# A fused attention and gated-MLP kernel: its build-time scheduler places single instructions event by event instead of whole steps

## The chip, the cores and the metric

The kernel runs on one core of one Trainium2 chip. The metric is the device time of one execution in microseconds (us). The execution that was profiled is one such execution; its span runs from the first to the last instruction of the program and is a little shorter than its device time.

## The reference

The input x has 2048 tokens (S) of width 640 (D). After a layer norm over D, two branches read the same xn and both are added to x:

- attention in linear form with 32 heads of width 20: q, k and v from one weight `wqkv`; q and k each go through a small per-head matrix `w_phi`, then through a softmax over +p and one over -p, which are laid side by side (40 features a head);
- a gated MLP of inner width 1536 (F).

```python
pq = einsum("bhsd,hdf->bhsf", q, w_phi);  pk = einsum("bhsd,hdf->bhsf", k, w_phi)
phi_q = concat([softmax(pq), softmax(-pq)]);  phi_k = concat([softmax(pk), softmax(-pk)])
kv  = einsum("bhsf,bhsd->bhfd", phi_k, v);    z = sum over s of phi_k
o   = (phi_q @ kv) / ((phi_q . z) + 1e-6)
out = x + concat_heads(o) @ wo + (silu(xn @ w1) * (xn @ w3)) @ w2
```

So kv and z are sums over all 2048 tokens of the k side, and nothing of the q side can be finished before they are complete.

## The kernel before

Tokens lie in 16 tiles of 128 (t = 0 to 15) and in 4 blocks of 512 (b = 0 to 3). The program is one list of steps per engine, laid out when it is built. The steps, with the names that the trace uses:

- **norm** of tile t: two `bn_stats` and one `bn_aggr` on VectorE (DVE), eps and the power on GpSimd (POOL), the scaling of `x_tok` on DVE or ScalarE (ACT). Tiles 0 to 3 are transposed by TensorE (PE), tiles 4 to 15 by a DMA transpose on SP's queue (`xnT<-x_tok`).
- **fold(1)** and **fold(0)**: `w_phi` is multiplied into the k and q weights (`PS<-BDc,wqkT`), five pieces each; the results are `Wkp` and `Wqp`. POOL builds `BDc` from `phi_s`.
- **V** and **K** of tile t: 10 matmuls of 320 columns each (`PS<-wv,xnT`, `PS<-Wkp,xnT`). V is copied by ACT into `v2`; K goes through two Exp on ACT into `ekt`.
- **k_norm** of tile t: DVE sums (`S<-ekt`) and takes reciprocals (`rS<-S`), POOL multiplies (`ekt<-ekt,rS`, two instructions). `S` and `rS` have three buffers.
- **kv_sum**: 192 small matmuls over all 16 tiles (`PS<-ekt,v`), then a copy to `kvT`; **kv_back**: 24 small matmuls (`PS<-PT,kvT`), then `KVc` on DVE. Only then can attention go on.
- **Q** of block b, piece fc: 5 matmuls of 512 columns (`PS<-xnT,Wqp`), two Exp on ACT (`EqT`).
- **q_tok** of tile t: 20 small matmuls into four PSUM banks (`PS<-KVc,EqT`), two `e_s` copies on ACT, then six instructions on DVE (`pr_s`, `den_s` twice, `g_s`, `prod`, `o_tok`), then a DMA transpose to `oT`.
- **M** of block b, piece fc (48 in all): 10 matmuls of 512 columns into two banks (`PS<-xnT,w_s`; `w_s` stands for w1, w3 and w2 alike), a Tanh on ACT (`th`), two `scalar_tensor_tensor` on DVE (`t`, `hT`).
- **O** of tile t: 34 matmuls of 320 columns (`PS<-wo_s,oT` and `PS<-w_s,hT`), one add on DVE (`xres`), a store.

What sets the order: `_Program` keeps a modelled clock per engine. Nine streams (norms, x_dma, attention, k_norms, o_transposes, mlps, outs, stores, x_loads) offer one step each; the loop picks the step whose modelled start is earliest, `commit` appends **all** instructions of that step to their engines' lists, and the choice starts anew. PSUM banks are chosen by `banks(n)` as an aligned group of n, and a group is free when the last reader of any of its banks has ended. An engine runs its list strictly in order: an instruction that stands behind a waiting one waits too. PE starts with 21 dummy matmuls on a zero tile (`dummies`), before the first real work. Nearly every instruction is recorded by one helper, so the profile shows them all at line 104.

Of the kernel before, what the change touches and what calls it, by code (L numbers as in the profile page):

```python
# [9 lines left out]
D = 640  # L10
# [10 lines left out]
ENGINES = ("PE", "ACT", "DVE", "POOL", "SP")  # L21
GRAN = 32

# [5 lines left out]
TRIPLES = ((0, 3, 0, 60), (3, 3, 60, 60), (6, 3, 120, 60), (9, 3, 180, 60), (12, 3, 240, 60), (13, 3, 300, 20))  # L29


class _Op:
    __slots__ = ("name", "part", "eng", "emit", "reads", "writes", "cost", "dma", "deps", "start", "end",
                 "inc", "count", "sem", "clock", "idx")

    def __init__(self, eng, emit, reads, writes, cost, dma=False):
        self.eng, self.emit, self.reads, self.writes = eng, emit, reads, writes
        self.cost, self.dma = cost, dma
        self.name = ""
        self.part = False  # L40
        self.inc = False
        self.count = 0
        self.sem = None


class _Program:

    def __init__(self, nc):  # L50
        self.nc = nc
        self.eng = {"PE": nc.tensor, "ACT": nc.scalar, "DVE": nc.vector,
                    "POOL": nc.gpsimd, "SP": nc.sync}
        self.base = {}
        self.ops = []
        self.free = dict.fromkeys(ENGINES, 0.0)
        self.bus = 0.0
        self.last_w = {}
        self.last_r = {}
        self.bank = {}  # L60
        self.pending = None
        self.pool = None
# [6 lines left out]
    def regions(self, ap):  # L69
        if not hasattr(ap, "ap"):  # L70
            return []
        name = ap.name
        esz = mybir.dt.size(ap.dtype)
        dims = [list(d) for d in ap.ap]
        row = dims[0][0]
        off = ap.offset % row
        if name == self.psum:
            span = off + sum(s * (n - 1) for s, n in dims[1:])
            if len(dims) == 3 and (dims[1][0] * esz) % 2048 == 0:
                step = dims[1][0] * esz // 2048  # L80
                return [("P", off * esz // 2048 + step * i) for i in range(dims[1][1])]
            return [("P", k) for k in range(off * esz // 2048, span * esz // 2048 + 1)]
        if name not in self.base:
            return []
# [8 lines left out]
        b = self.base[name]  # L93
# [3 lines left out]
        return list(g)  # L97

    def op(self, eng, name, writes, reads, args, kw=None, cost=0.1):
        m = getattr(self.eng[eng], name)  # L100
        kw = kw or {}
        w = [g for a in writes for g in self.regions(a)]
        r = [g for a in reads for g in self.regions(a)]
        o = _Op(eng, lambda: m(*args, **kw), r, w, cost)  # L104
        o.name = name + ":" + ",".join(a.name for a in writes)
        o.part = eng == "POOL" and any(a.start_partition() != 0 for a in writes)
        self.pending.append(o)
        return o

    def dma(self, eng, out, in_):  # L110
        m = self.eng[eng].dma_start
        nbytes = 1
        for n in out.shape:
            nbytes *= n
        nbytes *= mybir.dt.size(out.dtype)
        o = _Op(eng, lambda: m(out, in_), self.regions(in_), self.regions(out), nbytes, True)  # L116
        o.name = "dma:" + out.name
        self.pending.append(o)
        return o

    def dma_t(self, eng, out, in_):
        m = self.eng[eng].dma_start_transpose
        nbytes = 2
        for n in out.shape:
            nbytes *= n
        o = _Op(eng, lambda: m(out, in_), self.regions(in_), self.regions(out), nbytes * 1.4, True)
        o.name = "dmat:" + out.name
        self.pending.append(o)
        return o

    def find_deps(self, o):
        deps = {}

        def add(d):
            k = ("dma", d.idx) if d.dma else d.eng
            if k not in deps or deps[k].idx < d.idx:
                deps[k] = d

        e = o.eng
        if e == "POOL" and self.pool is not None and (o.part or self.pool.part):  # L140
            add(self.pool)
        for g in o.reads:
            if isinstance(g, tuple):
                for d in self.bank.get(g, {}).values():
                    if d.eng != e:
                        add(d)
                continue
            d = self.last_w.get(g)
            if d is not None and not (d.eng == e == "PE"):
                add(d)  # L150
        for g in o.writes:
            if isinstance(g, tuple):
                for d in self.bank.get(g, {}).values():
                    if d.eng != e:
                        add(d)
                continue
            d = self.last_w.get(g)
            if d is not None:
                add(d)
            for d in self.last_r.get(g, {}).values():  # L160
                if d.dma or o.dma or d.eng != e or e == "POOL":
                    add(d)
        return list(deps.values())

    def ready(self, ops):

        t, off = 0.0, 0.0
        for o in ops:
            if o.eng != "PE":
                continue  # L170
            for d in self.find_deps(o):
                t = max(t, d.end + 0.07 - off)
            off += o.cost
        return t

    def start_of(self, o):
        return max([self.free[o.eng]] + [d.end + 0.07 for d in self.find_deps(o)])

    def commit(self, ops):
        for o in ops:  # L180
            o.idx = len(self.ops)
            o.deps = self.find_deps(o)
            t = self.free[o.eng]
            for d in o.deps:
                t = max(t, d.end + 0.07)
            o.start = t
            if o.dma:
                self.free[o.eng] = t + 0.06
                self.bus = max(self.bus, t + 0.4) + o.cost / 280e3
                o.end = self.bus + 1.6  # L190
            else:
                o.end = t + o.cost
                self.free[o.eng] = o.end
            self.ops.append(o)
            if o.eng == "POOL" and not o.dma:
                self.pool = o
            for g in o.reads:
                if isinstance(g, tuple):
                    self.bank.setdefault(g, {})[o.eng] = o
                else:  # L200
                    self.last_r.setdefault(g, {})[("dma", o.idx) if o.dma else o.eng] = o
            for g in o.writes:
                if isinstance(g, tuple):
                    self.bank.setdefault(g, {})[o.eng] = o
                else:
                    self.last_w[g] = o
                    self.last_r.pop(g, None)

    def step(self, build):
        self.pending = []  # L210
        build()
        p, self.pending = self.pending, None
        return p

    def emit(self, finish):
        nc = self.nc
        sem = {e: nc.alloc_semaphore("s_" + e) for e in ENGINES}
        for o in self.ops:
            for d in o.deps:
                d.inc = True  # L220
        count = dict.fromkeys(ENGINES, 0)
# [3 lines left out]
        for o in self.ops:  # L225
# [10 lines left out]
            if o.dma:  # L236
# [13 lines left out]
        return lists  # L250


def bass_parallel_sum__linear_kernel_hedgehog__glu_gated_swiglu__prompt_kernel(
# [81 lines left out]

# [12 lines left out]
    P.psum = PS[:].name  # L348
# [7 lines left out]
    def mm(o, l, r, start, stop, shared=False, cost=None):  # L356
        n = 1
        for k in r.shape[1:]:
            n *= k
        P.op("PE", "matmul", [o], [l, r], (o, l, r),  # L360
             dict(start=start, stop=stop, skip_group_check=shared),
             cost=max(n / 2400 + 0.0025, 0.035) if cost is None else cost)

    def tr(o, i):
        P.op("PE", "transpose", [o], [i, ident[:]], (o, i, ident[:]), cost=0.056)

# [6 lines left out]
    def act(o, i, f, scale=1.0):  # L373
        P.op("ACT", "activation", [o], [i], (o, i, f), dict(scale=scale),
             cost=0.17 + free(o) / 1200)
# [557 lines left out]
```

## Time and profile before

| | |
|---|---|
| device time, median of 3 runs | 288.65 us (288.58, 288.65, 290.89) |
| the profiled execution | 290.46 us, its span 288.7 us |
| mean granted TensorE clock | 0.970 |
| busy PE / DVE / ACT / POOL | 273.2 / 183.8 / 103.0 / 61.4 us |

A group of instructions shows its busy time and the mean duration of one. Matmuls overlap in the pipeline, so the time that a group of matmuls takes on PE is read from the start of one group to the start of the next, not from the durations. "Idle before" is the time in which the engine had nothing to run just before the row, with what ended it. [...]

### The profile page before, as it was taken

What the parts mean: (1) busy time and instruction counts of PE and PEld (TensorE: products, weight loads), DVE (VectorE), ACT (ScalarE), POOL (GpSimd) and SP (SyncE); (2) the same over time, 40 slices, a digit from 0 to 9 for tenths busy, and PEclk for the clock granted to TensorE, in tenths of its full rate; (3) what the DMA queues carried; (4) which work ended last, traced back from release to release, by engine and by line L of the source; (5) the groups of instructions that cost most, each with busy time, mean ns of one, the idle gap of its engine ahead of it and who ended that gap; (6) DMA issues with size and microseconds to landing.
All of it is one profiled execution on the core that took longest, in us unless ns stands there. A gap on an engine that the chain in (4) does not pass through costs nothing.

```text
span 288.7 us, 5054 instructions
## 1 busy us (share of the span) xinstructions
PE 273.2 (95%) x2081; PEld 160.8 (56%) x2081; DVE 183.8 (64%) x308; ACT 103.0 (36%) x191; POOL 61.4 (21%) x101
## 2 busy tenths in 40 slices
PE   7599999799999999999974999999999999999996
PEld 3376576576444444444463444445666667777774
DVE  3439776999766666666682689989555567761212
ACT  3267895776822222232200354454232220000000
POOL 4503157999950000000036000000000000000000
PEclk9599999999999999999995799999999999999999
DMA  7994597720000000000026011111322323332201
GB/s 205 243 356 156 101 260 144 187 89 2 0 0 0 2 0 0 0 2 1 0 35 242 0 39 33 25 23 23 70 72 68 91 70 92 92 93 81 73 31 45
DMA packets 40311, 21.98 MB, mean 76 GB/s; under 512 B 26720, under 2 KB 40288, under 8 KB 40288
## 3 DMA queue, kind: packets, MB, share of 16 engines
q1 hardware_dynamic: 40288, 21.66, 28.7%
q8 instruction: 16, 0.26, 0.4%
q14 instruction: 7, 0.06, 0.1%
HBM read 12.81 MB, written 2.62 MB: 53 GB/s over the span
## 4 chain that ended last, share of the span: by engine, by line
PE 82%; POOL 5%; DVE 5%; ACT 3%; DMA 2%; issue 1%; SPq 1%; POOLq 1%; ACTq 0%
PE PS L104 82%; DVE bst L104 2%; POOL ekt L104 2%; DMA x_tok<-in_A_x_dram 2%; ACT ekt L104 2%; ACT x_tok L104 1%; POOL v L104 1%; SPq L116 1%; POOL PT L104 1%; ACT th L104 1%; DVE S L104 1%; DVE mv L104 1%; POOL mv L104 1%; DVE t L104 0%; POOLq L884 0%
## 5 line engine op out<-in xcount | busy, mean ns | idle before, releaser
L104 PE MATMUL PS<-xnT,w_s 128*128 128x512 bf16 x480 | 107.2, 384 | 0.0
L104 PEld LDWEIGHTS PS<-xnT,w_s 128*128 128x128 bf16 x480 | 47.3, 99 | 57.2 <-issue 2.2
L104 DVE SCALAR_TENSOR_TENSOR t<-th,PS 128x512 bf16<-128x512 f32 x48 | 33.0, 687 | 34.7 <-ACT th L104 34.7
L104 PE MATMUL PS<-w_s,hT 128*128 128x320 bf16 x384 | 54.9, 299 | 0.0
L104 POOL TENSOR_TENSOR ekt<-ekt,rS 128x640 bf16<-128x640 bf16 x32 | 39.4, 1274 | 65.2 <-DVE rS L104 65.1
L104 ACT ACTIVATE th<-PS 128x512 f32<-128x512 f32 x48 | 28.7, 599 | 59.7 <-PE PS L104 59.7
L104 PEld LDWEIGHTS PS<-w_s,hT 128*128 128x128 bf16 x384 | 37.6, 98 | 14.6
L104 DVE TENSOR_TENSOR xres<-PS,xres 128x640 bf16<-128x640 f32 (+1 forms) x17 | 13.4, 786 | 42.3 <-PE PS L104 42.3
L104 DVE SCALAR_TENSOR_TENSOR hT<-t,PS 128x512 bf16<-128x512 bf16 x48 | 33.0, 687 | 2.3 <-PE PS L104 0.6
L104 PE MATMUL PS<-wv,xnT 128*128 128x320 bf16 x160 | 26.3, 316 | 0.7 <-ACT ekt L104 0.7
L104 ACT ACTIVATE EqT<-PS 128x512 bf16<-128x512 f32 x40 | 21.6, 596 | 10.8 <-PE PS L104 10.8
L104 PE MATMUL PS<-wo_s,oT 128*128 128x320 bf16 x160 | 24.6, 300 | 0.0
L104 DVE TENSOR_TENSOR prod<-PS,g_s 128x1280 bf16<-128x1280 f32 x16 | 23.9, 1491 | 0.6
L104 PE MATMUL PS<-Wkp,xnT 128*128 128x320 bf16 x160 | 23.9, 299 | 0.0
L104 PE MATMUL PS<-xnT,Wqp 128*128 128x512 bf16 x100 | 23.8, 381 | 0.0
L104 ACT ACTIVATE e_s<-PS 128x64 f32<-128x64 f32 x32 | 7.7, 284 | 43.5 <-PE PS L104 43.5
L104 DVE TENSOR_REDUCE S<-ekt 128x64 f32<-128x1280 bf16 x16 | 23.1, 1446 | 0.0
L104 ACT ACTIVATE ekt<-PS 128x640 bf16<-128x640 f32 x32 | 20.7, 705 | 5.6 <-PE PS L104 5.6
L104 PEld LDWEIGHTS PS<-wv,xnT 128*128 128x128 bf16 x160 | 16.1, 103 | 7.8 <-ACT ekt L104 0.9
L104 PEld LDWEIGHTS PS<-wo_s,oT 128*128 128x128 bf16 x160 | 15.3, 98 | 7.0
L104 PEld LDWEIGHTS PS<-Wkp,xnT 128*128 128x128 bf16 x160 | 15.7, 98 | 6.2
L104 DVE BATCH_NORM_STATS2 bst<-x_tok 128x6 f32<-128x320 bf16 x32 | 15.3, 479 | 5.1 <-DMA x_tok<-in_A_x_dram 4.6
(57 smaller groups left out, 152.1 us busy)
## 6 DMA issues: line engine op xcount, KB each, us to landing
w_s<-in_B_w_dram SPq DMA_DIRECT2D x6, 640.0 KB, 6.4
xres<-in_A_x_dram SPq DMA_DIRECT2D x16, 160.0 KB, 2.2
out_dram<-xres SPq DMA_DIRECT2D x15, 160.0 KB, 1.8
x_tok<-in_A_x_dram SPq DMA_DIRECT2D x3, 640.0 KB, 11.1
w_s<-in_B_w_dram SPq DMA_DIRECT2D x1, 1920.0 KB, 8.1
wv<-in_A_wqkv_dram SPq DMA_DIRECT2D x2, 400.0 KB, 4.7
wo_s<-in_A_wo_dram SPq DMA_DIRECT2D x1, 800.0 KB, 5.1
x_tok<-in_A_x_dram SPq DMA_DIRECT2D x2, 160.0 KB, 2.3
```

The source lines that it names most:

```text
L104: o = _Op(eng, lambda: m(*args, **kw), r, w, cost)
L116: o = _Op(eng, lambda: m(out, in_), self.regions(in_), self.regions(out), nbytes, True)
```

## The change

`_Program` is written anew. All instructions are recorded first (`P.all`) with their data dependences; a matmul group and its PSUM banks form a `_Unit`, and `schedule` then places one instruction at a time: of PE's ready units and of the ready instructions of ACT, DVE, POOL and SP it commits the one that can start first, and among those that could start at once the one of the highest level. A unit's four, two or one banks are waited for one by one, each against the readers of its last owner (`bank_time`), instead of as a group. A q_tok unit may not be placed before the `prod` of the tile before it has been placed (`turned`, `behind`). The levels are written as due times (`when`). The computation and the shapes of its matmuls stay; only dummy matmuls are added, and in O the MLP's chunks now come ahead of the attention's. Copies that ACT or DVE can do are given to either when they are placed.

```diff
+    def schedule(self, start, filler=None, filler_until=0.0):
...
+        def bank_time(i, off, guess):
+            u, j = p
+            for r in u.readers[j]:
+                if r.done:
+                    t = max(t, r.end + SEM["PE"])
...
+                for u in sorted(ready_u, key=lambda u: (-u.level, u.mms[0].idx)):
+                    for k in range(0, 8, u.banks):
+                        g = group_time(u, k)
+                        if g < 1e8:
+                            opts.append((max(g, u.at), fit(k, u.banks, u.at), k))
+                    if opts:
+                        x = min(opts)
+                        if pick is None or x[0] < pick[0] - (0.03 + MODE):
+                            pick = (x[0], u, x[2])
...
+            for e in ("ACT", "DVE", "POOL", "SP"):
+                ts = [(max(free[e], op_time(o, e)), o) for o in ready[e]]
+                t = min(x[0] for x in ts)
+                t, o = min((x for x in ts if x[0] <= t + 0.03), key=lambda x: (-x[1].level, x[1].idx))
+                if best is None or t < best[0]:
+                    best = (t, e, o, None)
...
     def q_tok(t, level):
+        u = P.begin(4, level, "row", "qt")
+        u.behind.extend(turned[-1:])
...
-        chunks = [(oT[:, i, t * 128:(t + 1) * 128], wo_s, i) for i in range(DC)]
-        chunks += [(hT[b][:, i, ti * 128:(ti + 1) * 128], w2_s, i) for i in range(FC)]
+        chunks = [(hT[b][:, i, ti * 128:(ti + 1) * 128], w2_s, i) for i in range(FC)]
+        chunks += [(oT[:, i, t * 128:(t + 1) * 128], wo_s, i) for i in range(DC)]
...
-    def dummies():
-        for i in range(9):
-            mm(bank(7), zero[:, 0:128], zero[:], True, True, False, 0.427)
-        for i in range(12):
-            mm(bank(7, 128), zero[:, 0:128], zero[:, 0:128], True, True, False, 0.056)
+    def filler(t, until):       # called whenever PE has a gap of over 0.25 us before 12 us
+        while t < until:
+            n = 512 if until - t > 0.5 else 128
...
+    load_x(0, 1, lv)
+    for q in range(2):
+        load(wv[:, :, 320 * q:320 * q + 320], ...)
+        load_x(q + 1, q + 2, lv - 3 - 2 * q)
+    load_x(3, 4, lv - 6)
+    load(phi_s[:], phi_t, lv - 7)
+    for e in range(DC):
+        load_wT(1, e, lv - 8 - e)
+    load_x(4, 8, lv - 19)
+    load_w13(0, 512, lv - 20)
...
+    for t in range(T):
+        if t >= 4:
+            v_tile(t, when(20 + 5.0 * (t - 4)))
+        k_tile(t, when(13 + 1.4 * t) if t < 4 else when(22 + 5.0 * (t - 4)))
+        k_norm(t, 1e3 - 10 * t)
...
+    kv_sum(when(100))
+    kv_back(when(0))
+    for fc in range(FC):
+        mlp(3, fc, when(300 + fc))
+    for b in range(NB):
+        for j in range(4):
+            q_tok(t, when(110 + t))
...
+    P.schedule({"PE": 1.25, "ACT": 2.1, "DVE": 0.93, "POOL": 0.8, "SP": 0.81}, filler, 12.0)
```

Three places show how instructions move. The first is DVE's list around kv_sum. Before, the sums of the last three k_norms stand behind a run of M instructions (`t`, `hT`); `kvT` is the copy that follows kv_sum:

```order
L104 SCALAR_TENSOR_TENSOR t_70<-th,PS 128x512
L104 SCALAR_TENSOR_TENSOR hT_73<-t_70,PS 128x512
L104 TENSOR_REDUCE S_63<-ekt 128x64
L104 RECIPROCAL rS_64<-S_63 128x64
L104 TENSOR_SCALAR kvT<-PS,epsc 128x2x80
```

Now the last k_norm stands 18 rows of M instructions ahead of that copy, right after the M that follows the last K:

```order
L552 RECIPROCAL rS_64<-S_63 128x64 [waits s_POOL,s_DVE]
L552 SCALAR_TENSOR_TENSOR hT_78<-t_70,PS 128x512 [waits s_PE,s_DVE]
L552 TENSOR_REDUCE S_63<-ekt 128x64 [waits s_ACT]
L552 SCALAR_TENSOR_TENSOR t_70<-th,PS 128x512 [waits s_ACT]
L552 RECIPROCAL rS_64<-S_63 128x64 [waits s_POOL,s_DVE]
L552 SCALAR_TENSOR_TENSOR hT_78<-t_70,PS 128x512 [waits s_PE,s_DVE]
```

The last of these reciprocals is that of tile 15. On POOL the big fill of `v2` (`MEMSET v_85`) moved with it, from ahead of all 32 `ekt` multiplications to just ahead of the last two.

The second place is DVE's list at the start, tiles 0 to 3. Before, the scaling of tile 1 (the second TENSOR_SCALAR) stands behind both `bn_stats` of tile 2; d5 is the load of tiles 2 and 3 together:

```order
L104 TENSOR_SCALAR x_tok<-x_tok,mv 128x640 [waits s_POOL]
L104 BN_STATS bst<-x_tok 128x6 [waits d5]
L104 BN_STATS bst<-x_tok 128x6 [waits s_DVE]
L104 BN_AGGR mv<-bst 128x2 [waits s_DVE]
L104 TENSOR_SCALAR x_tok<-x_tok,mv 128x640 [waits s_POOL]
```

Now tile 0's scaling stands behind tile 1's statistics (d3 is tile 1's load), and tile 1's behind one half of tile 2's and one of tile 3's (d5, d6):

```order
L552 BN_STATS bst<-x_tok 128x6 [waits d3]
L552 BN_STATS bst<-x_tok 128x6 [waits s_DVE]
L552 TENSOR_SCALAR x_tok<-x_tok,mv 128x640 [waits s_POOL]
L552 BN_AGGR mv<-bst 128x2 [waits s_DVE]
L552 BN_STATS bst<-x_tok 128x6 [waits d5]
L552 BN_STATS bst<-x_tok 128x6 [waits d6]
L552 TENSOR_SCALAR x_tok<-x_tok,mv 128x640 [waits s_POOL]
```

The third place is PE from kv_back (`PS<-PT,kvT`) on. Before, the small matmuls of kv_back follow kv_sum at once, and one M stands between them and the first q_tok:

```order
L104 MATMUL PS<-PT,kvT 64x21
L104 MATMUL PS<-xnT,w_s 128x512 x10
L104 MATMUL PS<-KVc,EqT_77 128x88 x20
L104 MATMUL PS<-xnT,Wqp 128x512 x10
L104 MATMUL PS<-xnT,w_s 128x512 x10
```

Now one M stands between kv_sum and kv_back and three stand behind it. Further down, the fifth to the eighth q_tok have one to three M units between them and few Q:

```order
L544 MATMUL PS<-KVc,EqT_84 128x88 x20
L544 MATMUL PS<-xnT,w_s 128x512 x10
L544 MATMUL PS<-xnT,Wqp 128x512 x5
L544 MATMUL PS<-xnT,w_s 128x512 x10
L544 MATMUL PS<-KVc,EqT_84 128x88 x20
L544 MATMUL PS<-xnT,w_s 128x512 x20
L544 MATMUL PS<-KVc,EqT_84 128x88 x20
L544 MATMUL PS<-xnT,w_s 128x512 x30
L544 MATMUL PS<-KVc,EqT_84 128x88 x20
L544 MATMUL PS<-xnT,Wqp 128x512 x15
```

Before, Q, M, M stood between nearly all of the first q_tok. The 12 M of block 3, which shared this stretch before, now run in one piece behind O of tile 11.

## Rows read from the trace of the kernel before

**Rows 1.** The page's head, and the granted TensorE clock in its 40 slices.

```profile
span 288.7 us, 5054 instructions
...
PEclk9599999999999999999995799999999999999999
```

**Rows 2.** The page's chain that ended last, shares of the span.

```profile
PE 82%; POOL 5%; DVE 5%; ACT 3%; DMA 2%; issue 1%; SPq 1%; POOLq 1%; ACTq 0%
```

**Rows 3.** What PE waited for: us in total, times, longest us.

```profile
PE PS L104 <- POOL ekt L104: 5.4, 3, 2.0
...
PE PS L104 <- ACT v L104: 1.1, 1, 1.1
PE PS L104 <- ACT ekt L104: 0.7, 1, 0.7
PE PS L104 <- ACT kvT L104: 0.6, 1, 0.6
```

**Rows 4.** PE at the start: start us, us, what, count [idle before <-releaser].

```profile
5.89 0.45 PE L104 MATMUL PS<-ident,x_tok 128*128 128x128 bf16 x5
10.15 0.71 PE L104 MATMUL PS<-ident,x_tok 128*128 128x128 bf16 x5 [3.81 <-DVE x_tok L104]
...
16.24 2.88 PE L104 MATMUL PS<-wv,xnT 128*128 128x320 bf16 x20
...
20.68 2.32 PE L104 MATMUL PS<-xnT,w_s 128*128 128x512 bf16 x10
```

**Rows 5.** DVE and POOL at the start, the same columns.

```profile
3.10 1.02 DVE L104 BATCH_NORM_STATS2 bst<-x_tok 128x6 f32<-128x320 bf16 x2 [1.88 <-DMA x_tok<-in_A_x_dram]
...
8.52 1.02 DVE L104 BATCH_NORM_STATS2 bst<-x_tok 128x6 f32<-128x320 bf16 x2 [2.69 <-DMA x_tok<-in_A_x_dram]
...
9.71 0.39 DVE L104 TENSOR_SCALAR x_tok<-x_tok,mv 128x640 bf16<-128x640 bf16 x1
...
12.29 2.05 POOL L104 TENSOR_TENSOR BDc<-phi_s,GF 128x140 bf16<-128x140 bf16 x5
```

**Rows 6.** Stretches: length, busy us (instructions) of PE, PEld, DVE, ACT, POOL; granted clock; DMA.

```profile
10.10:15.30 5.20, 5.14 (x26) 3.35 (x27) 1.95 (x5) 2.29 (x4) 3.53 (x9) 0.50 0.97 274
...
152.00:158.40 6.40, 2.32 (x48) 2.00 (x48) 1.13 (x3) 0.66 (x1) 4.46 (x5) 0.50 0.71 252
158.40:162.10 3.70, 3.70 (x15) 1.36 (x12) 1.65 (x3) 0.60 (x1) 0.00 (x0) 0.50 0.00 0
```

**Rows 7.** The chain around kv_sum and to the end: start us, us, what.

```profile
146.60 1.49 DVE S L104
...
148.75 4.95 POOL ekt L104 x4
...
157.57 128.52 PE PS L104 x1083
...
286.12 0.49 DVE xres L104
```

**Rows 8.** PE in the later stretches, columns as in Rows 4.

```profile
69.70 1.52 PE L104 MATMUL PS<-Wkp,xnT 128*128 128x320 bf16 x10
71.06 5.56 PE L104 MATMUL PS<-xnT,Wqp 128*128 128x512 bf16 x25
76.46 69.23 PE L104 MATMUL PS<-xnT,w_s 128*128 128x512 bf16 x320
145.62 4.00 PE L104 MATMUL PS<-ekt,v 128*64 128x120 bf16 x156
```

**Rows 9.** One q_tok on PE and on DVE, and the M instruction after it on DVE.

```profile
173.44 0.57 PE L104 MATMUL PS<-KVc,EqT 64*128 64x88 bf16 x20
...
174.43 0.22 DVE L104 TENSOR_TENSOR pr_s<-e_s 128x64 f32<-128x64 f32 x1
...
175.55 1.49 DVE L104 TENSOR_TENSOR prod<-PS,g_s 128x1280 bf16<-128x1280 f32 x1
...
177.49 0.68 DVE L104 SCALAR_TENSOR_TENSOR t<-th,PS 128x512 bf16<-128x512 f32 x1
178.20 0.69 DVE L104 SCALAR_TENSOR_TENSOR hT<-t,PS 128x512 bf16<-128x512 bf16 x1
```

**Rows 10.** POOL: the big fill of `v2`, and multiplications of k_norm in a row.

```profile
49.08 2.55 POOL L104 MEMSET v<- 128x512 bf16 x2
...
59.08 11.10 POOL L104 TENSOR_TENSOR ekt<-ekt,rS 128x640 bf16<-128x640 bf16 x9
```

More of the change, by code (lines that the diff above doesn't have):

```diff
@@ L21, with __init__ @@
 ENGINES = ("PE", "ACT", "DVE", "POOL", "SP")
+SEM = {"PE": 0.06, "ACT": 0.04, "DVE": 0.04, "POOL": 0.08, "SP": 0.05}
+MODE = 0.097
 GRAN = 32
+BACKLOG = 2.5
 def heads_of_chunk(c):
     return (128 * c) // DH, (128 * c + 127) // DH
-TRIPLES = ((0, 3, 0, 60), (3, 3, 60, 60), (6, 3, 120, 60), (9, 3, 180, 60), (12, 3, 240, 60), (13, 3, 300, 20))
 class _Op:
[L33 to L38, printed above, removed]
-        self.name = ""
[L40 to L43, printed above, removed]
+    __slots__ = ("ways", "eng", "emit", "raw", "war", "bankd", "succ", "unit", "ismm", "start", "end", "inc", "sem",
+                 "clock", "idx", "part", "level", "off", "done", "nbytes", "busy", "left", "name", "deps", "gates")
+    def __init__(self, ways):
+        self.ways = ways
+        self.eng = next(iter(ways)) if len(ways) == 1 else None
+        self.raw, self.war, self.bankd, self.succ = set(), set(), set(), []
+        self.unit = None
+        self.ismm = self.inc = self.part = self.done = False
+        self.sem = None
+        self.nbytes = 0
+        self.level = 0.0
+        self.off = 0.0
+        self.name = ""
+        self.gates = []
+class _Unit:
+    def __init__(self, banks, level, mode):
+        self.banks, self.level, self.mode, self.k = banks, level, mode, None
+        self.mms = []
+        self.first = {}
+        self.readers = [[] for _ in range(banks)]
+        self.behind = []
+        self.name = ""
 class _Program:
@@ L69, in regions @@
     def regions(self, ap):
-        if not hasattr(ap, "ap"):
-            return []
-        name = ap.name
+        if not hasattr(ap, "ap") or ap.name not in self.base:
+            return ()
         esz = mybir.dt.size(ap.dtype)
         dims = [list(d) for d in ap.ap]
[L75 to L84, printed above, removed]
+        off = ap.offset % dims[0][0]
+        key = (ap.name, esz, off, str(dims[1:]))
+        if key in self.cache:
+            return self.cache[key]
         runs = [off]
@@ L110, in dma @@
[L110 to L156, printed above, removed]
+        self.cache[key] = g
@@ L176, in start_of @@
[L176 to L185, printed above, removed]
+                o.raw.add(d)
+        for g in w:
+            d = self.last_w.get(g)
+            if d is not None:
+                o.raw.add(d)
+            o.war.update(self.last_r.get(g, ()))
@@ new lines, in add, with mm @@
+        for s in (o.raw, o.war):
+            s.discard(o)
+        o.level = level
+        for g in r:
+            self.last_r.setdefault(g, set()).add(o)
+        for g in w:
+            self.last_w[g] = o
+            self.last_r.pop(g, None)
+        self.all.append(o)
+        return o
+    def mm(self, emit, reads, bank, busy, cols):
+        o = _Op({"PE": (emit, busy, cols / 2400 + 0.17)})
+        o.unit, o.ismm = self.unit, True
+        self.unit.first.setdefault(bank, o)
+        self.unit.mms.append(o)
+        self.add(o, [], reads)
+        if self.unit.prev is not None and len(self.unit.mms) == 1:
+            o.war.add(self.unit.prev.mms[-1])
+        return o
@@ new lines, in op, with dma @@
+    def op(self, ways, writes, reads, banks=None, level=0.0, after=()):
+        o = _Op(ways)
+        if banks is not None:
+            o.unit = self.unit
+            for b in banks:
+                self.unit.readers[b].append(o)
+            after = list(after) + [self.unit.mms[-1]]
+        return self.add(o, writes, reads, level, after)
+    def dma(self, eng, emit, writes, reads, nbytes, busy=0.45, level=0.0, after=()):
+        o = _Op({eng: (emit, busy, 0.0)})
+        o.nbytes = nbytes
+        return self.add(o, writes, reads, level, after)
@@ L194, in commit @@
+            o.done = True
             self.ops.append(o)
[L195 to L199, printed above, removed]
[L200 to L207 removed]
@@ L209, in step @@
[L209 to L213, printed above, removed]
+            if e == "POOL" and not o.nbytes:
+                if pool_prev is not None and (o.part or pool_prev.part):
+                    o.raw.add(pool_prev)
+                pool_prev = o
+            for u in o.gates:
+                u.missing -= 1
+                if not u.missing:
+                    ready_u.append(u)
+            for s in o.succ:
+                if s.ismm:
+                    s.unit.missing -= 1
+                    if not s.unit.missing:
+                        ready_u.append(s.unit)
+                else:
+                    s.left -= 1
+                    if not s.left:
+                        for f in s.ways:
+                            ready[f].append(s)
@@ new lines, in unit_time, with op_time @@
+        def unit_time(u):
+            t = max([d.end for d in u.behind], default=0.0)
+            for o in u.mms:
+                for d in o.raw:
+                    if not (d.ismm and d.unit is u):
+                        t = max(t, d.end + (0.0 if d.eng == "PE" else SEM["PE"]) - o.off)
+            return t
+        def op_time(o, e):
+            t = 0.0
+            for d in o.raw:
+                t = max(t, d.end + SEM[e])
+            for d in o.war:
+                t = max(t, d.end + SEM[e] if d.eng != e or e == "POOL" or d.nbytes or o.nbytes else d.start)
+            if o.nbytes:
+                t = max(t, bus - BACKLOG)
+            return t
@@ new lines, in way, with emit, sb, add @@
+    def way(eng, name, args, kw, busy, lat):
+        u = P.unit
+        e = {"ACT": nc.scalar, "DVE": nc.vector, "POOL": nc.gpsimd}[eng]
+        def emit():
+            return getattr(e, name)(*[at(a, u) for a in args], **{k: at(v, u) for k, v in kw.items()})
+        return eng, (emit, busy, lat)
+    def sb(*aps):
+        return [a for a in aps if hasattr(a, "ap")]
+    def add(ways, w, r, banks=None, level=0.0, after=(), part=False):
+        o = P.op(dict(ways), sb(*w), sb(*r), banks, level, after)
+        o.part = part
+        return o
@@ new lines, in select, with load @@
+    def select(o, base, pattern, cm, cmp, fill, level=0.0):
+        n = free(o)
+        add([way("POOL", "affine_select", (), dict(out=o, in_=o, compare_op=cmp, fill=fill, base=base,
+                                                   pattern=pattern, channel_multiplier=cm),
+                 0.2 + n / 960, 0.25 + n / 960)], [o], [o], None, level, part=o.start_partition() != 0)
+    queue = {"SP": nc.sync, "ACT": nc.scalar}
+    def load(o, i, level=0.0, eng="SP", after=()):
+        n = mybir.dt.size(o.dtype)
+        for s in o.shape:
+            n *= s
+        return P.dma(eng, lambda: queue[eng].dma_start(o, i), sb(o), sb(i), n, 0.45, level, after)
```

861 lines of the change are left out of this document (460 added, 401 removed).

## The prediction

> **What bounds the kernel now.** I read the page's head and the chain's shares first. PE is on 82% of the chain, and in the 40 slices of the span the granted clock is below 9 only at the start and in slices 22 and 23 [rows 1, 2]. [...] The list of PE's waits then says how little there is: 5.4 us on POOL's `ekt`, 1.1 on ACT's `v`, 0.7 on ACT's `ekt`, 0.6 on `kvT`, in seven waits [rows 3], and 3.81 us at the start before the transposes of tile 1 [rows 4]. There is no wait of any note behind kv_back: the chain from 157.57 to 286.12 is PE alone, 1083 instructions, and then one DVE add [rows 7]. Last come the windows. PE's clock is 0.50 from 10.1 to 15.3 and from 152 to 162.1 [rows 6]. Three places, then: the start, V and K of one tile, and kv_sum.
>
> **The change, part by part.** The sum is made for the profiled execution: 290.46 us, a span of 288.7 and 1.76 around it.
>
> *kv_sum.* Before, its last matmuls wait for the last `ekt` of POOL. The chain shows why: the sums of those k_norms start on DVE at 146.60, behind the M instructions, and POOL's four multiplications at 148.75 take 4.95 [rows 7]. The order now has these k_norms ahead of some 27 us of M and Q on PE (ten M at ten matmuls or 2.16, five Q at five or 1.08), against some 9 us from the last K to the last `ekt`: two Exp on ACT (an estimate, 1.5), sums and reciprocal (146.60 to 148.75, 2.15 [rows 7]), two multiplications of 1.23 and the moved fill of `v2`, 2.55 [rows 10], and a hand-over or two. So the 5.4 goes. The 0.6 for `kvT` is covered by the M that now stands between kv_sum and kv_back (2.16). With the gaps the drop of the clock goes: PE is busy for 2.32 us in one window and 3.70 in the next at half clock [rows 6], and half of these 6.0 is lost, 3.0. Together 9.0. Lower bound 6.0, if the clock drops all the same; what would have to be late for none of it to go is a rival below.
>
> [...]
>
> *V and K.* The waits of 1.1 and 0.7 [rows 3] are ACT behind POOL's fill of `v2` (2.55 from 49.08 [rows 10]), which now stands ahead of the last two multiplications. 1.8 goes, lower bound 0.
>
> *The start.* The point that counts is where the M or K work begins without further waits: 20.68 before [rows 4]. The loads that end at 8.52 bring the same bytes as before, so this time stays. Tile 1 has a load of its own now, which ends by interpolation between 3.1 and 8.5 (half of the bytes) at about 5.5. Its statistics (1.02 [rows 5]) no longer wait for those of tile 2, but its scaling stands behind one half of the statistics of tiles 2 and 3, which wait for the last load: 8.5 + 0.5 + 0.4 [rows 5] = 9.4 for its transposes, against 10.15. That is a gain of 0.7 only; the wait remains. Behind it, tile 2's scaling needs the other two halves (four in all, 2.04), one scaling (0.39) and POOL's multiplications, before which `BDc` (2.05) may stand [rows 5]: 8.5 + 2.04 + 0.39 + 2.05 = 13.0, with a hand-over 13.1. Then remain the transposes of tiles 2 and 3 (0.5) and what stood between 16.24 and 20.68, 20 matmuls of V and the folds [rows 4], 4.4: 18.0 in all. This is shorter than before because V's first halves and some folds fill the waits. Lower bound 17.0, without `BDc` in the way and with more of the folds in the gaps; upper 20.7, nothing gained.
> I assume that the clock is up by then: the 37 fillers (12 of 512 and 10 of 128 first) keep PE busy to about 12 us, where the 21 dummies ended before 5.89 and left the 3.81 open. The clock in the page is 0.50 from 10.1 to 15.3 [rows 6], after that gap.
>
> *From there on.* Before, 286.09 − 20.68 = 265.4 to the last matmul [rows 4, 7]. Less 9.0 and 1.8: 254.6. What hides the order change here is PE's own length, so the question is whether DVE can follow. Behind kv_back three M now come before the first q_tok, and that costs nothing: the same M count stands elsewhere.
>
> *One attention tile in flight.* This is the added wait. A q_tok of PE takes 0.57, and then DVE works from 174.43 (`pr_s`) to 177.49, when M's `t` may start: a block of 3.06, in which `prod` is 1.49 [rows 9]. An M asks DVE for 0.68 + 0.69 = 1.4 [rows 9] against 2.16 of PE. While DVE is in the block, an M's two banks stay full. From the fifth q_tok to the eighth the order has seven M and one Q: on PE 3 × 0.57 + 7 × 2.16 + 1.08 = 17.9 us, on DVE 3 × 3.06 + 7 × 1.37 = 18.8. DVE is 0.9 longer in that stretch; later the q_tok are wider apart. I take 1.0 for such stalls; lower 0 (before showed none with nearly the same work); upper 6.6, if four tiles each stall by the block less what two full banks give PE to do meanwhile, 3.06 − 1.4 = 1.66 (1.4 is M's 2.16 less the 0.76 until its own `t` could start, an estimate). The choice is nearer to 0 because the nearest row, PE's chain of 128.52 without a wait [rows 7], had the same 16 blocks, though closer to their neighbours in M and Q.
>
> *O.* MLP chunks first and attention last needs no more PE time; `xres` after the last matmul is 0.49, the tail to the end stays 2.6. The output store is as before. `xT` by DMA of tiles 4 to 7 now stands ahead of two weight loads on SP's queue; the tiles are wanted from about 28 us, and I cost it at nothing, covered by some microseconds of slack. If the cover is gone, it is a rival (E).
>
> Sum: 18.0 + 254.6 + 1.0 + 2.6 = 276.2 of span; + 1.76 = **278.0 us**, 12.5 less than the profiled 290.46. The median of the runs shown, 288.65, lies 1.8 below the profiled execution, and no row says where. Two of three runs were near 288.6; one was 290.89. From the median the same step would give 276.2. I forecast **277.0** between the two.
>
> **The rivals.**
> - *B, the start keeps a low clock.* If the transposes of tile 1 at 9.4 leave gaps of about 1 us around them, the work from 8.6 to 15.4 may again run at 0.50, as it did from 10.1 to 15.3 [rows 6], 3.5 us more at most: 280 to 281. For it: fillers of 128 columns with waits between. Against it: PE is never idle for long before 12 us.
> - *C, attention becomes DVE's.* The upper bound above: four to six q_tok each 1.66 late, 4 to 6.6 more than the 1.0 taken: 282 to 284. For it: the 18.8 against 17.9. Against it: before, the same blocks stood under 128.52 us of PE without a wait [rows 7], and each stalled tile leaves more room to the next.
> - *D, slower: DVE waits for POOL.* `S` and `rS` have three buffers. If in the stage of V and K DVE reaches a reciprocal while POOL still holds the third `rS`, DVE stands, M's banks behind it stay full, and PE stands. POOL needs 11.10 / 9 = 1.233 for a multiplication [rows 10], 2.47 a tile; PE needs 1.36 each for V and K [rows 8] and 2.16 for an M, 4.88 a tile, so POOL is fast enough by half as long as each tile has an M. It decides from two tiles of k_norm close behind each other on, as where a piece of POOL's other work (2.55 for the fill [rows 10]) stands between: the wait is then two tiles, 4.93, less what the banks cover, 1.4, so 3.5 each time. With one for every second tile of tiles 4 to 14, five, it is 17.7, and the time 294 to 296. Against it: the order has an M for nearly each tile, and the fill stands at the end.
> - *E, the plan does not hold.* The places are chosen on modelled times. If loads land later than modelled, PE waits in its strict order for V of tile 4 or for a weight. The row for a late x_tok is 3.81 [rows 4]; with two or three such waits most of the 12.5 is given back and it ends at about 287. Against it: the loads have the same bytes and the same queue.
>
> **How the numbers follow.** Forecast, with terms at or near the values taken (274 to 281 by the start's bounds, 1.0 less or 2.7 more, and the 1.8 between executions): 0.62. B with the rest as forecast 0.14, C 0.12, D 0.05, E 0.07. The range takes in the forecast, B and most of C, 273 to 285. A measurement of this kernel tells about 1% from no change: 285.8 to 291.5. Faster by over 1%: forecast, B and C, 0.88. Within 1%: E, 0.07. Slower by over 1%: D, 0.05.
>
> **What would show it.** In the profile of the changed kernel: kv_sum is one row of 192 matmuls with no POOL `ekt` among PE's waits, and the clock is 9 in every slice after the first one or two. The first M or K starts at 17 to 19, with one wait on `x_tok` that ends near 9.4. DVE's waits for `PS` in attention leave PE at most some 0.5 us at a time, 1.0 in total, none of it before kv_back. The prediction is wrong if PE waits for `x_tok` or a weight after 20 us, if DVE's `pr_s` or `prod` stands as PE's releaser for more than 3 us, or if POOL's `rS` readers end late and DVE waits for them in the K stage.

## The result, and the profile after

| | before | after |
|---|---|---|
| device time, median | 288.64 us (4 runs, 288.58 to 290.89) | 277.38 us (4 runs, 277.26 to 277.50) |
| profiled execution, span | 290.46, 288.7 us | 277.50, 275.8 us |
| mean granted clock | 0.970 | 0.999 |

The ratio over all runs is 0.959 (95% interval 0.9545 to 0.9638; between the medians it is 0.961). 277.0 was forecast. The page's head and its clock row, which answer to [rows 1]:

```profile
span 275.8 us, 5050 instructions
...
PEclk9999999999999999999999999999999999999999
```

All that PE waited for (us in total, times, longest), which answers to [rows 3]:

```profile
PE PS L544 <- DMA wqkT<-in_A_wqkv_dram: 1.3, 2, 0.7
PE PS L946 <- DVE warm L552: 1.3, 1, 1.3
PE PS L544 <- DVE hT L552: 0.5, 1, 0.5
PE PS L706 <- DVE x_tok L552: 0.2, 1, 0.2
```

The waits on POOL's `ekt`, on `v`, on `kvT` are gone; a new one on `wqkT` is there. PE at the start (start us, us, what, count [idle before]), which answers to [rows 4]:

```profile
6.97 0.45 PE L706 MATMUL PS<-ident,x_tok 128*128 128x128 bf16 x5 [0.19 <-DVE x_tok L552]
...
8.97 0.45 PE L706 MATMUL PS<-ident,x_tok 128*128 128x128 bf16 x5
...
11.78 0.45 PE L706 MATMUL PS<-ident,x_tok 128*128 128x128 bf16 x5
12.07 0.36 PE L544 MATMUL PS<-BDc,wqkT 128*128 128x140 bf16 x4
13.13 0.23 PE L544 MATMUL PS<-BDc,wqkT 128*128 128x140 bf16 x1 [0.71 <-DMA wqkT<-in_A_wqkv_dram]
13.95 0.23 PE L544 MATMUL PS<-BDc,wqkT 128*128 128x140 bf16 x1 [0.57 <-DMA wqkT<-in_A_wqkv_dram]
14.02 0.44 PE L706 MATMUL PS<-ident,x_tok 128*128 128x128 bf16 x5
...
18.27 5.60 PE L544 MATMUL PS<-Wkp,xnT 128*128 128x320 bf16 x40
```

The first K starts at 18.27. Ahead of it the first fold stands at 12.07 and waits twice for a piece of `wqkT`; tile 3's transposes, behind it in the list, start only at 14.02. The stretch around kv_sum, same columns, which answers to [rows 7, 8]:

```profile
106.54 4.88 PE L544 MATMUL PS<-ekt,v 128*64 128x120 bf16 x192
111.35 2.33 PE L544 MATMUL PS<-xnT,w_s 128*128 128x512 bf16 x10
113.62 0.60 PE L544 MATMUL PS<-PT,kvT 128*64 128x84 bf16 x24
114.15 6.65 PE L544 MATMUL PS<-xnT,w_s 128*128 128x512 bf16 x30
...
144.86 1.25 PE L544 MATMUL PS<-xnT,w_s 128*128 128x512 bf16 x5 [0.47 <-DVE hT L552]
```

All 192 matmuls of kv_sum run in one piece of 4.88 us. Before, the same work and kv_back took from 145.62 to 158.4. The last row is the only wait of the attention stretch. The profiled executions differ by 12.9 us of span: the point where the startup work ends moved from 20.68 to 18.27 (2.4), the time from there to the last matmul went from 265.4 to 273.13 − 18.27 = 254.9 (10.5), the tail stayed (2.61 and 2.67).

### The profile page after: what moved, and what is told of

It is laid out like the page before. It is cut to its first block, busy times and chain, and to the rows that moved or that the text cites. A ratio compares the mean times of both kernels' runs of the same rounds, so it can differ in the third digit from the quotient of the medians.

```text
span 275.8 us, 5050 instructions
## 1 busy us (share of the span) xinstructions
PE 269.9 (98%) x2097; PEld 159.1 (58%) x2097; DVE 178.2 (65%) x311; ACT 101.7 (37%) x188; POOL 60.6 (22%) x101
## 4 chain that ended last, share of the span: by engine, by line
PE 91%; SPq 3%; ACT 2%; DMA 1%; issue 1%; DVE 1%
PE PS L544 91%; SPq L612 2%; ACT EqT L552 2%; DMA wqkT<-in_A_wqkv_dram 1%; SPq L606 1%; DVE hT L552 0%; DVE den_s L552 0%; DVE xres L552 0%; ACT e_s L552 0%; PE PS L706 0%; DVE pr_s L552 0%; DVE g_s L552 0%; DVE prod L552 0%; DVE t L552 0%
## 5 line engine op out<-in xcount | busy, mean ns | idle before, releaser
L544 PE MATMUL PS<-xnT,w_s 128*128 128x512 bf16 x480 | 108.4, 379 | 0.5 <-DVE hT L552 0.5
L544 PEld LDWEIGHTS PS<-xnT,w_s 128*128 128x128 bf16 x480 | 46.3, 98 | 54.2 <-DVE hT L552 1.0
L552 DVE SCALAR_TENSOR_TENSOR hT<-t,PS 128x512 bf16<-128x512 bf16 x48 | 32.4, 674 | 1.4 <-PE PS L544 0.4
L552 ACT ACTIVATE EqT<-PS 128x512 bf16<-128x512 f32 x40 | 21.7, 594 | 12.5 <-PE PS L544 12.5
L544 PE MATMUL PS<-wv,xnT 128*128 128x320 bf16 x160 | 24.9, 299 | 0.0
L552 ACT ACTIVATE e_s<-PS 128x64 f32<-128x64 f32 x32 | 9.1, 284 | 37.8 <-PE PS L544 37.3
L544 PEld LDWEIGHTS PS<-wv,xnT 128*128 128x128 bf16 x160 | 15.3, 98 | 7.3
L552 ACT ACTIVATE v<-PS 128x640 bf16<-128x640 f32 (+1 forms) x19 | 11.3, 595 | 16.5 <-PE PS L544 16.2
```

The costliest lines, as they stand in the source:

```text
L544: return nc.tensor.matmul(o(u.k), l, r, start=start, stop=stop, skip_group_check=shared)
L552: return getattr(e, name)(*[at(a, u) for a in args], **{k: at(v, u) for k, v in kw.items()})
```

## The experiments

Each kernel is the changed one with the edit shown, or the kernel before where its heading says so. The first kind is compared with the changed kernel's 277.38, and each ratio is taken over all runs to the kernel before, run beside it, so that it can differ a little from that of the medians. The kernel before had medians of 290.07, 289.99 and 289.56 in the three sets of runs, and a wide spread in each (286.87 to 291.01 over all).

**The last three k_norms late** (e1). Their 12 instructions are put back behind the M ahead of kv_sum; PE's list is untouched.

```diff
...
+    late = set(held_back)          # the ops of k_norm for t = 13, 14, 15
+    late_ops = [o for o in P.ops if o in late]
+    P.ops = [o for o in P.ops if o not in late]
+    n = next(i for i, o in enumerate(P.ops) if o.ismm and any(d in late for d in o.unit.mms[-1].raw))
+    P.ops[n:n] = late_ops
```

> The changed kernel with one thing put back: the sums, reciprocals and multiplications of the last three k_norms stand on DVE and POOL behind the M instructions ahead of kv_sum; PE's list is unchanged. Theory (the gain at kv_sum came from these k_norms being early, and the drop of the clock from the waits): the sums start near 106.5 us, the last multiplication ends near 106.5 + 2.0 + 6 x 1.23 = 115.9, so kv_sum ends some 4.8 us later, in gaps of at most 2 us, and the clock falls to 0.50 behind them for another 1.5 to 3 us: 283.7 to 285.3 us. If the clock drop has another cause than such short gaps, it stays at full rate: 282.2. Rival (the gain came from the order as a whole, and PE finds other work): under 279.

285.5 us (284.75 to 286.29), 8.1 more, 0.2 above the theory's range. PE around kv_sum:

```profile
112.18 0.47 PE L544 MATMUL PS<-ekt,v 128*64 128x120 bf16 x12 [0.96 <-POOL ekt L552]
114.63 0.75 PE L544 MATMUL PS<-ekt,v 128*64 128x120 bf16 x12 [1.98 <-POOL ekt L552]
117.09 0.75 PE L544 MATMUL PS<-ekt,v 128*64 128x120 bf16 x12 [1.71 <-POOL ekt L552]
117.77 4.15 PE L544 MATMUL PS<-xnT,w_s 128*128 128x512 bf16 x10
121.85 0.60 PE L544 MATMUL PS<-PT,kvT 128*64 128x84 bf16 x24
```

The stretches behind the gaps (length, busy us and count of PE, PEld, DVE, ACT, POOL; granted clock, DMA, GB/s):

```profile
113.00:115.00 2.00, 0.37 (x8) 0.37 (x10) 0.96 (x2) 0.00 (x0) 2.00 (x3) 0.92 1.02 367
115.00:117.00 2.00, 0.38 (x10) 0.22 (x6) 0.00 (x0) 0.00 (x0) 2.00 (x2) 0.50 1.07 375
...
119.00:121.00 2.00, 2.00 (x6) 0.76 (x5) 0.25 (x1) 0.60 (x1) 0.00 (x0) 0.50 0.00 0
```

The old waits are back, 4.6 us, and with them the lower clock: 0.92 from 113 to 115, 0.50 from there to 121, and the M behind takes 4.08 us to the next row instead of 2.27. Nothing in PE's list had changed, so both belong to the late k_norms: 4.6 + 1.8, and 1.1 in the matmuls of kv_sum itself (10.55 us from its start to the M less 4.65 of waits, against 4.81), which run in four pieces, the last two of them slower: 0.75 us for 12 matmuls instead of 0.47. Another 0.7 lies ahead of kv_sum, which starts at 107.22 in this execution; PE's list has one wait of 0.5 on a DMA transpose (`xnT<-x_tok`) here, which the changed kernel does not have.

**The same part alone, in the kernel before** (e2). The 12 instructions are moved up behind the first M after the last K.

```diff
...
+    P.ops = rest[:n] + early + rest[n:]   # k_norm of t = 13, 14, 15, ahead of the second M behind K of tile 15
```

> The kernel before with one part of the change alone: its last three k_norms moved up on DVE and POOL to the place behind the first M after the last K; every other list is as it was. Theory: the waits on ekt (5.4) and the half clock (3.0) go, the waits at the start, at V and K and for kvT stay: 288.6 - 8.4 = 280.2 us (279.5 to 281). If the clock drop has another cause than the waits, 283.2. Rival (most of the 11.3 us comes from the new order as a whole): over 285.

281.67 us against 290.07 in the same set, 8.4 less; ratio 0.9714 (0.9674 to 0.9754). The difference is the 8.4 expected; the time lies above the expected 279.5 to 281, which was worked out from 288.6. PE's waits and kv_sum:

```profile
PE PS L104 <- DVE x_tok L104: 3.8, 1, 3.8
...
PE PS L104 <- ACT v L104: 1.1, 1, 1.1
PE PS L104 <- ACT ekt L104: 0.7, 1, 0.7
PE PS L104 <- ACT kvT L104: 0.7, 1, 0.7
```
```profile
146.01 4.98 PE L104 MATMUL PS<-ekt,v 128*64 128x120 bf16 x192
151.68 0.60 PE L104 MATMUL PS<-PT,kvT 128*64 128x84 bf16 x24 [0.69 <-ACT kvT L104]
152.22 2.33 PE L104 MATMUL PS<-xnT,w_s 128*128 128x512 bf16 x10
```

Twelve instructions in another place give about seven tenths of what the whole change gives (2.9% of 4.1%), and the order of PE did not have to move for it. The M behind kv_sum takes 2.26 us to the next q_tok, where before, at a granted clock of 0.50 [rows 6], it took 4.07:

```profile
158.46 4.13 PE L104 MATMUL PS<-xnT,w_s 128*128 128x512 bf16 x10
162.53 0.56 PE L104 MATMUL PS<-KVc,EqT 64*128 64x88 bf16 x20
```

**No fillers, and fillers up to the first transposes only** (e3, e4).

```diff
-    P.schedule({...}, filler, 12.0)
+    P.schedule({...}, filler, 0.0)     # e3; 6.0 in e4
```

> The changed kernel without any filler matmuls: PE is idle until the first transposes at 7 us. Theory (fillers hold the clock up): PE runs at 0.50 for the first part of its 8.3 us of real start work, and the first K starts 3 to 5 us later: 280.4 to 282.4. Rival (the start is bound by loads, the clock there is hidden): 277.4, within 0.5.

> The changed kernel with fillers only up to the first transposes, so that gaps of about 1 us stay open between 7 and 12 us. Theory (only longer idle time costs the clock): 277.4, within 0.5. Rival B of the prediction (gaps of 1 us with small work between them bring the clock down): 0.50 for some us of the start, 279 to 281.

277.18 (276.96 to 277.79) and 277.29 us (277.28 to 277.43): the fillers are worth nothing that shows. The start without them:

```profile
7.14 0.71 PE L706 MATMUL PS<-ident,x_tok 128*128 128x128 bf16 x5 [7.14 <-DVE x_tok L552]
8.65 1.52 PE L544 MATMUL PS<-wv,xnT 128*128 128x320 bf16 x5 [0.80 <-ACT xnT L552]
...
18.56 1.66 PE L544 MATMUL PS<-Wkp,xnT 128*128 128x320 bf16 x11
```

Five matmuls of V take 1.52 us, where after 8.22 in the changed kernel they take 0.85: by these durations PE does run at about half speed there. But at 13.71 five transposes take 0.44, as in the changed kernel (0.45), where at 7.14 they took 0.71: full speed again, about when the last piece of `wqkT` lands (13.95 in the changed kernel), and the first K comes at 18.56, only 0.3 later. My theory for e3 (3 to 5 us) fell; that for e4 held.

**The transposing loads on ACT's queue** (e5).

```diff
...
-        load_wT(1, e, lv - 8 - e)
+        load_wT(1, e, lv - 8 - e, "ACT")   # and SP's first transpose waits for them
```

> The changed kernel with the five transposing loads of the k weights (wqkT) issued by ACT, which is idle then, rather than by SP behind eight other loads; the scheduler places the rest anew. Theory (the start is bound by these loads: in the changed kernel's trace SP issues them from 4.29 to 11.7 us and two folds wait for them until 13.95): the folds no longer wait, and the first K's work is done 0.7 to 2 us sooner: 275.4 to 276.7 us. Rival (the start is bound by x: load, statistics, scaling, transposes, as the prediction's sum had it): 277.4, within 0.5; or worse, if the transposes now slow the loads of x.

The edit also makes the sums of each k_norm wait for the reciprocal of three tiles before. 282.2 us (281.87 to 282.96), 4.8 more. PE, and ACT where it issues the fourth piece:

```profile
22.70 0.23 PE L544 MATMUL PS<-BDc,wqkT 128*128 128x140 bf16 x1 [1.02 <-DMA wqkT<-in_A_wqkv_dram]
...
27.55 4.65 PE L544 MATMUL PS<-Wkp,xnT 128*128 128x320 bf16 x33
```
```profile
10.80 0.44 ACT L552 ACTIVATE v<-PS 128x320 bf16<-128x320 f32 x1 [8.50 <-PE PS L544]
10.81 1.16 ACTq L612 DMA_TRANSPOSE wqkT<-in_A_wqkv_dram  x1
```

The first three transposing loads, issued by 5.58, now run beside the loads of x, and tile 1's statistics start at 7.45, against 5.54 before the edit. That is the rival's last clause. But the other two are issued only at 10.81 and 14.46, each directly behind a copy of V on ACT, and these copies wait for the late x. The last piece lands some 8.2 us after its issue, and PE waits for it until 22.70. So the edit did not bring `wqkT` early, as it was meant to: the run shows tile 1's statistics 1.91 us later with these loads beside those of x, and not what `wqkT` in time would be worth.

**The first loads in the old order** (e6), tiles 2 and 3 in one load, tile 1 ahead of `wv`.

```diff
+    load_x(1, 2, lv - 1)
...
-        load_x(q + 1, q + 2, lv - 3 - 2 * q)
-    load_x(3, 4, lv - 6)
+    load_x(2, 4, lv - 6)
```

> The changed kernel with the first loads in the order of before: x tile 0, x tile 1, both halves of wv, x tiles 2 and 3 together. Prediction's sum (the start gains by tile 1's statistics and the order on DVE, set by when x lands): up to 0.7 us slower, 277.4 to 278.1. Theory from the trace after (wqkT is the bound, and SP now has one load less to issue, 0.43 us, ahead of it): 276.9 to 277.4.

277.36 us (277.10 to 277.58). The order of these loads carries no gain.

**Several attention tiles in flight** (e7).

```diff
-        u.behind.extend(turned[-1:])
```

> The changed kernel without the rule that a q_tok may not be placed before prod of the tile before it. Theory (PE's list is long enough either way and DVE follows): 277.4, within 0.5; the one wait of 0.47 on hT may go or move. Rival (the rule is what keeps two blocks of 3.06 us from standing on DVE in a row, while M's banks stay full): 1.4 to 1.66 us for each pair placed close together, 279 to 284.

304.36 us (303.16 to 305.21), 27.0 more, and slower than the kernel before: ratio 1.0495 (1.0452 to 1.0538). Both theories fell, the rival in size. PE's waits, and the first of the places:

```profile
PE PS L544 <- DVE den_s L552: 8.0, 3, 2.7
PE PS L544 <- DVE prod L552: 6.9, 3, 2.6
PE PS L544 <- DVE pr_s L552: 2.5, 1, 2.5
PE PS L544 <- DVE hT L552: 1.3, 3, 0.5
```
```profile
131.07 0.61 PE L544 MATMUL PS<-KVc,EqT 64*128 64x88 bf16 x21
132.20 0.56 PE L544 MATMUL PS<-KVc,EqT 64*128 64x88 bf16 x19 [0.51 <-DVE hT L552]
135.21 3.19 PE L544 MATMUL PS<-xnT,Wqp 128*128 128x512 bf16 x14 [2.45 <-DVE pr_s L552]
```
```profile
120.00:190.00 70.00, 50.20 (x471) 23.96 (x476) 54.96 (x112) 29.69 (x70) 0.00 (x0) 0.84 0.21 36
```

Two q_tok stand next to each other and hold all eight banks, four each. No unit can start, whatever it is, until DVE has gone through the first block: seven times, up to 2.75 us each. The last row, the window from 120 to 190, says what comes on top: the granted clock is 0.84 in the mean, and matmuls between such gaps are slower too: the ten matmuls of the M at 174.02 take 3.94 us to the next row, those of the M at 156.62 take 2.25. The waits sum to about 19, and the rest of the 27 is of the size of the clock's loss (an estimate: 0.16 of 70 us, 11 at most).

**Banks freed as a group** (e8), in the plan and in the waits.

```diff
-            for r in u.readers[j]:
+            for r in [r for rs in u.readers for r in rs]:
...
+                        for rs in p[0].readers:
+                            x.mms[0].bankd.update(rs)
```

> The changed kernel with the banks of a unit freed as a group, in the plan and in the waits, as before: the first matmul waits until every reader of all the banks' last owners has ended. Theory (before, PE ran 128.5 us without a wait on groups): 277.4, within 0.7. Rival (banks one by one are needed for M, whose two banks come free some 0.7 to 1.4 us apart, and for q_tok's four): PE waits at many M or q_tok of the attention stretch, 0.1 to 0.3 us each over 30 units, 280 to 286.

278.15 us (277.91 to 278.67), 0.8 more, with one new wait of PE, 1.0 us, on `prod` ahead of a q_tok. The 0.5 on `hT` is gone in exchange. The first theory's bound was 278.1; the rival's 280 is not reached.

**The plan with the true landing times of `wqkT`** (e9).

```diff
+                o.end = max(bus + 1.35, lands.get(o, 0.0))   # 11.5, 12.0, 12.5, 13.3, 14.2 for wqkT
```

> The changed kernel with one number of its plan corrected: the five loads of wqkT are taken to land at 11.5, 12.0, 12.5, 13.3 and 14.2 us, about when they did, so that the transposes of tile 3 and three halves of V come ahead of the first fold on PE. Theory (PE's two waits for wqkT, 1.3 us, are open only because the fold stands ahead of work that is ready): the first K near 17.0 instead of 18.27, 276.0 to 276.6 us. Rival (another bound takes its place, tile 3's x or the copies of Wkp on ACT and DVE): 277.0 to 277.5.

277.63 us (277.34 to 277.70), no gain. The wait moved:

```profile
17.14 1.04 PE L545 MATMUL PS<-Wkp,xnT 128*128 128x320 bf16 x6
19.26 4.79 PE L545 MATMUL PS<-Wkp,xnT 128*128 128x320 bf16 x34 [1.07 <-DVE Wkp L553]
```

The folds stand close together now, K starts at 17.14, and waits 1.07 us for the last copies of `Wkp`. The rival's mechanism held, 0.1 above its range: 1.3 us of waits for `wqkT` were not 1.3 us of time.

**The fill of `v2` early** (e10) and **O's attention chunks first** (e12), each as before.

```diff
+        if t == 9:
+            ones_late()                 # e10, at a high level
...
+        chunks = [(oT[:, i, t * 128:(t + 1) * 128], wo_s, i) for i in range(DC)]    # e12
+        chunks += [(hT[b][:, i, ti * 128:(ti + 1) * 128], w2_s, i) for i in range(FC)]
```

> The changed kernel with the big fill of v2 on POOL put back among the V tiles (ahead of the copy of tile 9's V) instead of ahead of the last multiplications. Prediction's term (V and K): up to 1.8 us slower, 277.4 to 279.2. Rival (the plan puts the fill where POOL is idle, or M into the gap): 277.4, within 0.4.

> The changed kernel with the chunks of O in the order of before, the attention's ahead of the MLP's. Theory (the transposed o_tok lands long before O of its tile): 277.4, within 0.3. Rival (it lands late for the tiles of the stretch where O and q_tok alternate): PE waits on oT there, 278 to 281.

277.39 (277.13 to 277.65) and 277.55 us (277.44 to 278.23): no difference, twice. In e10 POOL fills `v2` at 46.51 to 48.9, among the V tiles, and the plan puts an M there on PE; no wait on `v` appears.

**Tile 1's scaling moved up, in the kernel before** (e11).

```diff
-            if t:
-                yield lambda t=t: ln_apply(t - 1)
+            if t == 1:
+                yield lambda: ln_apply(0)
+                yield lambda: ln_apply(1)
...
```

> The kernel before with one part of the change alone: tile 1's scaling on DVE ahead of the statistics of tile 2, so that PE's transposes of tile 1 do not wait until 10.15. PE's list is as before. Theory (the idle time of 3.98 us goes, and with it the half clock from 8.5 to 15.4): the first M starts 1 to 3 us sooner than 20.68, 286 to 287.6 us. Rival (the weights behind it bound the start: the load of phi and BDc end at 14.3 in the trace of before): 288.6, within 0.5.

288.77 us (10 runs, 287.42 to 290.74) against 289.56 (15 runs): ratio 0.9992 (0.9955 to 1.0028). The profiled execution shows the expected start:

```profile
11.04 0.45 PE L104 MATMUL PS<-ident,x_tok 128*128 128x128 bf16 x5 [2.15 <-DVE x_tok L104]
...
17.62 2.11 PE L104 MATMUL PS<-xnT,w_s 128*128 128x512 bf16 x9
```

The first M at 17.62 instead of 20.68, and clock 1.00 from 8.5 to 15.4. But runs of the kernel before come out like this without the edit: of the 29 in the three sets, ten have a mean clock of 0.970 and spans of 288.3 to 289.3, ten have 0.982 and 286.6 to 287.9, and the rest lie between or, once, above. An estimate from these means: 0.970 of 288.6 us is 17.3 us at 0.50, 0.982 of 287.0 is 10.3, with the rest at 1.00. The 7.0 between them is about the length of the stretch of 8.6 to 15.3 that stands at 0.50 in the profile before ([rows 6] and the row ahead of them, below). So the drop at the start may come and go by itself and cost some 1.7 us; whether it does was not profiled.

```profile
8.60:10.10 1.50, 0.00 (x0) 0.00 (x0) 1.43 (x5) 0.00 (x0) 0.22 (x1) 0.50 1.27 290
```

The edit moves the wait to tile 2 (2.15 us) rather than removing it. The time is the rival's, but not its reason, since the start did move; the size of the gain stays open, and the interval leaves at most about 1.3 us.

## Why the prediction was right, point by point

- **kv_sum, 9.0 us.** Right, cause and size. e1 puts 8.1 back, of which 7.5 lies at kv_sum, e2 alone takes 8.4 away, and both move waits and clock together. (The waits listed for the kernel before are six, not the seven counted.)
- **The clock behind the gaps at kv_sum.** Right. In e1 no gap there is over 1.98 us, and the granted clock is 0.50 from 115 to 121; in the changed kernel, without the gaps, it is 1.00 from 106 to 118. So gaps of at most 2.0 us [rows 3] between small matmuls were enough here.
- **V and K, 1.8 us.** The wait went, but for another reason. I said that the moved fill frees ACT; with the fill back among the V tiles (e10) nothing is lost. In e10's order an M stands on PE while POOL fills; I take it that this hides the fill, and no run took the M away.
- **The start, 18.0.** Measured 18.27, by a chain that was in part another. Tile 1's transposes came at 8.97 (9.4 said), tile 2's at 11.78 (13.1 said); what I did not see was that the first fold would wait for `wqkT` until 13.95 with the rest behind it. Tile 2 came 1.3 early and `wqkT` cost 1.3 of waiting, so the closeness of 18.27 to 18.0 is partly luck. Nor did a wait on `x_tok` end near 9.4: fillers and V's first half stood there, and PE waited 0.19 us in all. The chain of waits in the profile after:

```profile
4.29 1.60 SPq L612
...
9.07 1.27 SPq L612
...
10.38 3.52 DMA wqkT<-in_A_wqkv_dram
```

  SP needs 1.27 to 1.78 us to issue each of the five pieces, and the last takes 3.52 to land. I take it that four edges lie within about a microsecond of each other here: x, `wqkT`, V's matmuls, the copies of `Wkp`. It would explain why e3, e6 and e9 each moved one of them and not the time.
- **Rival B.** Its price was wrong: 3.5 us for a start at the lower clock, where e3 shows 0.3 for a stretch from 7.1 to some point before 13.7. PE had slack against the loads. The fillers, which the sum leaned on, could go.
- **One attention tile in flight, 1.0 us.** The added wait cost 0.47, on M's bank, of the kind that was said. But I treated the rule as a cost only. In this scheduler, which places whatever can start first, it holds q_tok apart; without it the changed kernel is 5% slower than the one before (e7). That was a second mechanism on the slower side, and none of my rivals named it.
- **The rest.** From the first K on, PE took 254.4 us and 0.47 of waiting (254.6 and 1.0 said); the tail 2.67 (2.6). An M's 2.16, ten matmuls of [rows 8], held: two M take from 23.71 to 28.02. Profiled against profiled, the step is 290.46 − 277.50 = 13.0, where 12.5 was said. The 1.8 us by which the profiled execution of before lay above the median goes with its mean clock, 0.970, against 0.982 in shorter runs (spans of 286.6 to 287.9 us in the three sets). The changed kernel has no such spread: 277.26 to 277.50. The forecast of 277.0 was set between 276.2 and 278.0 without knowing where the 1.8 came from. The sum was for the profiled execution (278.0, measured 277.50), and that 277.0 lies 0.4 from the median is in part luck. The cover of tile 4's DMA transpose, costed at nothing, held in the changed kernel and was thin: such a wait took 0.5 in e1 and 0.3 in e12.

None of the versions tried beats the changed kernel by more than its runs differ.

## What to carry to other kernels

PE, busy for 95% of the span before and 98% after, gave back its gaps and the time at the lower clock behind them. For such a kernel list the gaps, find for each the instruction that is late, and try that instruction alone in the old order before a new scheduler; here twelve instructions gave seven tenths of the gain. A greedy scheduler needs a rule for any unit that takes half of a shared resource: here two of them side by side closed it for everyone (27.0 us in e7). Where several chains may end within a microsecond, as at this start, taking one away may show little: e3, e6 and e9 lie within 0.25 us of the changed kernel.

## What was not expected of the hardware

- The granted clock reads 1.00 in e3's first 19 us, also where matmuls take 1.8 times as long (five of V in 1.52 us instead of 0.85):

```profile
7.00:9.00 2.00, 1.07 (x7) 0.69 (x8) 1.27 (x5) 0.70 (x1) 1.33 (x5) 1.00 1.31 157
```

  At this start the durations and that row do not agree: five transposes take 0.71 at 7.14, as they do before at a granted clock of 0.50 [rows 4, 6], and 0.44 at 13.71. Ahead of the slow ones PE was idle for 7 us.
- With three transposing loads on ACT's queue, issued by 5.58, a plain load on SP's that was issued at 1.73 in both programs came later: tile 1's statistics start at 5.54 in the changed kernel and at 7.45 in e5. The load of tiles 4 to 7 was issued at 5.05 there instead of 11.70, and no run tells the two apart.

```profile
5.54 1.02 DVE L552 BATCH_NORM_STATS2 bst<-x_tok 128x6 f32<-128x320 bf16 x2 [1.21 <-DMA x_tok<-in_A_x_dram]
```
```profile
7.45 1.02 DVE L552 BATCH_NORM_STATS2 bst<-x_tok 128x6 f32<-128x320 bf16 x2 [2.98 <-DMA x_tok<-in_A_x_dram]
```

  The first K came 9.3 us later in e5; the two late issues and two M ahead of it have a part in that.
